# Sliding-window attention and a GELU layer on one core: seven products in place of eight in part of the first layer, and other places for the attention's visits

## Chip, core and metric

The kernel runs on one core of a Trainium2 chip. The metric is the device time of one execution in microseconds. The core's engines are TensorE (matrix products, "PE" in the profile, its weight loads "PEld"), VectorE ("DVE"), ScalarE ("ACT"), GpSimd ("POOL") and SyncE ("SP", which here only issues DMA transfers).

## What is computed

Windowed attention over 8 batches of 576 positions with 8 heads of 64, then two dense layers with a tanh GELU between them, over all 4608 positions:

```python
scores = scale * np.matmul(q, k.transpose(0, 1, 3, 2))
mask = np.abs(pos[:, None] - pos[None, :]) <= 32
scores = np.where(mask, scores, -1000000000.0)
attn = np.exp(scores - np.max(scores, axis=-1, keepdims=True))
attn = attn / (np.sum(attn, axis=-1, keepdims=True) + 1e-09)
x = np.matmul(attn, v)              # then reshaped to (4608, 512)
h = x @ w_in                        # (4608, 2048)
g = 0.5 * h * (1.0 + np.tanh(c * (h + 0.044715 * h * h * h)))
out = g @ w_out                     # (4608, 512)
```

## The kernel before

The positions go through the dense layers in nine tiles of 512. Each tile t has a first product (`ffn_in`, line 541: x by w_in, 16 columns of 128 features, four matmuls of 512 positions each) and a second product (by w_out). `gelu` (line 549) takes each of the 16 results out of PSUM on ScalarE. Tile 0 computes its second product directly (`ffn_out_0`). Tiles 1 to 8 compute it by Strassen-Winograd's seven products in place of eight (`ffn_out`, line 639; the table `WINO` gives the order: A11, S2, A12, S3, S1, A22, S4). The S factors are sums and differences of quarters of the GELU's result and are made by `sums` (line 584), four VectorE operations after every fourth column. The results are added up on VectorE in `ffn_out` and `ffn_last`, and stored from POOL's queue.

While tile t runs, the attention of batch t + 1 is computed between the matmuls of its second product. This order is written out by hand: `PLAN_0` (tile 0), `PLAN_1` (tile 1) and `PLAN` (tiles 2 to 6) map a step i of the second product (one matmul a step, 112 of them) to actions that are issued ahead of it:

- `s` scores of a pair of heads and their exponential (`score`, lines 436 and 448); `@0`, `@1` name the PSUM tile. `s-1` and group 4 are the tail, the last positions of a batch.
- `m` the mask (`mask`, line 454, VectorE).
- `v` the row sums and the product with V (`weigh`, lines 459 and 469), then on ScalarE the logarithm and the exponential that invert the sums (lines 494 and 495).
- `x` the normalizing product into xT on VectorE (`spread`, lines 504 and 510), which the first product of the next tile reads.
- in tile 0 also `d` (a second copy of a piece of V at shifted positions, lines 198 and 200), `e` (the cast of a piece of V on POOL), `n` and `p` (row sums and product with V of two pairs of heads), `w` and `u` (casts of w_out).

Three of 16 columns of the next tile's first product are begun at the end of a tile and finished at the start of the next. Each engine works strictly through its own instructions in the order in which they are written; between engines there are semaphores. ScalarE loads a table for the exponentials and another for the GELU. Tile 7 has only the tail of the last batch left (steps 5 and 31), tile 8 no attention at all.

q and k come in by SP's queue, v by POOL's (by SP's for the first three batches); q and k are cast on VectorE at the start of a tile and turned by transposing transfers on SP's queue (`cast_and_turn`, lines 364 and 386) into QT and KT, which `s0` needs.

[...]two of `psM` (`bank(0)`, `bank(1)`), two pairs of `psS` (tags S0 and S1, two banks each in one tile), and O and D of `psO`. In tiles 1 to 8 column n of the first product goes to bank 0, to the pair S0 (n = 1, 2) or, by n modulo 3, to D, bank 1 or bank 0.

Of the kernel before, what the change touches and what calls it, by code (L numbers as in the profile page):

```python
# [9 lines left out]
FP32 = mybir.dt.float32  # L10
FP16 = mybir.dt.float16
AF = mybir.ActivationFunctionType
ALU = mybir.AluOpType
# [23 lines left out]
def cut(b):  # L37
# [5 lines left out]

PLAN = {4: "s0@0 s1@1 v-1", 16: "m0 m1 x-1", 33: "s2@0 v0@1 v1", 36: "m2", 44: "x0", 50: "x1",
        62: "s3@0 s4@1 v2", 66: "m3", 80: "x2", 84: "m4", 91: "v3", 112: "x3"}


# [1 line left out]


PLAN_0 = {4: "s0@0", 9: "r1@1", 14: "s1@0", 15: "w1", 16: "m0", 19: "k2", 22: "r2@1", 23: "m1", 25: "s2@0", 27: "t-1@1",
          29: "w2", 31: "s-1@1", 33: "n0@0", 35: "e0", 36: "m2", 37: "k3", 38: "w5", 39: "m-1", 40: "r3@1", 43: "e1",
          45: "s3@0", 46: "v-1@1 d0", 47: "w3 e2", 48: "m3", 50: "d1", 51: "n2@0 x-1", 52: "e3 e4 d2", 54: "d3 p0@0",
          55: "u3 p2@1 x0 x1", 56: "x2 x3", 60: "c1"}
PLAN_1 = PLAN | {10: "s0@0", 12: "s1@1", 33: "s2@0", 40: "v0@1 v1", 50: "x0", 53: "x1", 57: "s-1@1", 62: "s3@0 v2",
                 63: "m-1", 66: "m3", 73: "v-1@1", 76: "x2", 80: "x-1", 86: "v3", 90: "s4@1", 98: "m4"}
PLAN_1[16] = "m0 m1"
for i in (4, 44, 84, 91):  # L60
    del PLAN_1[i]
PAIR_1 = {17: slice(0, 4), 40: slice(4, 8)}

ORDER_0 = [(t4, 4 * w + i) for w in range(3) for i in ((0, 2, 3, 1), (0, 2, 1, 3), range(4))[w] for t4 in (0, 1, 3, 2)] + \
# [8 lines left out]
def kernel(  # L73
# [264 lines left out]
    def bank(i):  # L338

        return psM.tile([128, 512], FP32, name="mm", tag=f"x{i}")  # L340
# [75 lines left out]

    def score(b, g, pair):
        m, prs, steps, slots, q0, n = work_of(b, g)
        ps = psS.tile([128, 2, 512], FP32, name="ps_s", tag=f"S{pair}")
        added = b == 0 and g < 4  # L420
        if added:
            for half in range(2):
                for h in range(2):
                    r0 = 64 * h
                    nc.tensor.matmul(ps[64 * half:64 * half + 64, h, :], idn[r0:r0 + 64, r0:r0 + 64],
                                     bias[half][r0:r0 + 64, :, :], start=True, stop=False,
                                     skip_group_check=True)
        for r, pr in enumerate(prs):
            for step in steps:
                for half, piece in enumerate(step):  # L430
                    if piece is None:
                        continue
                    k0, p0, p1 = piece
                    for h in range(2):
                        r0 = 64 * h
                        nc.tensor.matmul(  # L436
                            ps[64 * half:64 * half + 64, h, 4 * n * r:4 * n * r + 4 * n].rearrange(
                                "k (j p) -> k j p", j=4)[:, :, p0 - q0:p1 - q0],
                            KTs[b % 2][r0:r0 + 64, pr, k0:k0 + 64] if k0 < 512 else
                            KLs[b % 2][r0:r0 + 64, pr, :],  # L440
                            QTs[b][r0:r0 + 64, pr, :, p0:p1], start=not added, stop=True,
                            skip_group_check=added)
        w = 4 * n * len(prs)
        pe = yp.tile([128, 2, w], FP16, name="pe", tag="yo") if (b, g) == (1, 3) else \
            hp.tile([128, 2, w], FP16, name="pe", tag="qt16") if (b, g) == (0, 3) else \
            pep.tile([128, 2, w], FP16, name="pe", tag="pe") if g < 4 else \
            tailp.tile([128, 2, w], FP16, name="pet")
        nc.scalar.activation(pe, ps[:, :, 0:w], AF.Exp, scale=SCALE)  # L448
        groups[(b, g)] = pe

    def mask(b, g, hs=slice(0, 2)):
# [95 lines left out]
    def gelu(t, n):  # L547
        fc = column(t, n)
        nc.scalar.activation(gTs[t][:, fc, :], phs[fc], AF.Gelu_apprx_tanh)  # L549
        if t and n % 4 == 3:  # L550
            sums(t, n // 4)

    wino = {}

    def combine_w():
# [53 lines left out]
    def ffn_out_0(t4, fc):  # L609
        new = t4 not in pys  # L610
        if new:
            pys[t4] = bank(t4) if t4 < 2 else psO.tile([128, 512], FP32, name="py3", tag="OD"[t4 % 2])
        nc.tensor.matmul(pys[t4], gTs[0][:, fc, t4 * 128:t4 * 128 + 128], w_out16[:, fc, :],
                         start=new, stop=(fc == NF - 1))
        if fc == NF - 1:
            if "yo" not in pys:
                pys["yo"] = hp.tile([128, 2, 512], FP32, name="yo2", tag="qt16")
            yo = pys["yo"][:, t4, :] if t4 < 2 else yp.tile([128, 512], FP32, name="yo", tag="yo")
            (nc.scalar.copy if t4 > 1 else nc.vector.tensor_copy)(yo, pys[t4])
            later.append((t4, yo))  # L620

    def ffn_out(t, i):

        n, blk, f = i // 16, i // 8 % 2, i % 8
        a, w, new = WINO[n]
        end = t == NT - 1
        if i % 16 == 0 and new:
            pys[n % 2] = bank((1 + n) % 2)
            if end and n == 4:
                pys["apart"] = psO.tile([128, 512], FP32, name="py2", tag="O")  # L630
        py = pys[n % 2].rearrange("p (b c) -> p b c", b=2)
        apart = end and blk and n in (4, 6)
        if a[0] == "A":
            r0, c0 = 8 * (int(a[2]) - 1) + f, 256 * (int(a[1]) - 1) + 128 * blk
            lhsT = gTs[t][:, r0, c0:c0 + 128]
        else:
            lhsT = wino[a][:, f, 128 * blk:128 * blk + 128]
        one = end and n in (4, 6)
        nc.tensor.matmul(pys["apart"][:, 0:256] if apart else py[:, blk, :], lhsT,  # L639
                         wino[w][:, f, :], start=(new and i % (8 if one else 16) == 0),  # L640
                         stop=(i % (8 if one else 16) == (7 if one else 15)),
                         skip_group_check=True)
        if i % 16 < 15:
            return
        yo, left, right = wino["yo"], slice(0, 256), slice(256, 512)
        C11, C12, C21, C22 = (yo[:, r:r + 2, c] for r in (0, 2) for c in (left, right))

        M1, U2, U3 = C21, C12, C22
        if n == 0:
            nc.vector.tensor_copy(M1, py)  # L650
        elif n == 1:
            nc.vector.tensor_tensor(U2, py, M1, op=ALU.add)
        elif n == 2:
            (nc.vector.tensor_copy if t > 1 else nc.scalar.copy)(C11, py)
            if end:
                for x in range(2):
                    store(t, x, yo[:, x, :], left, nc.sync)
        elif n == 3:
            nc.vector.tensor_tensor(U3, py, M1, op=ALU.add)
        elif n == 4:  # L660
            if not end:
                nc.vector.tensor_tensor(C22, py, U3, op=ALU.add)
            else:
                for x, part in enumerate((py[:, 0, :], pys["apart"][:, 0:256])):
                    nc.vector.tensor_tensor(C22[:, x, :], part, U3[:, x, :], op=ALU.add)
                    store(t, 2 + x, yo[:, 2 + x, :], right, nc.sync, nc.scalar)
        elif n == 5:
            nc.vector.tensor_tensor(C21, py, M1, op=ALU.add)  # L668
            for x in range(2):
                store(t, 2 + x, yo[:, 2 + x, :], *((left, nc.sync, nc.scalar) if end else ()))  # L670
# [142 lines left out]
    for t in range(NT):  # L813
        b = t + 1
        att = b < B
        if t:
            for fc in range(begun):
                ffn_in(t, fc, 3, 4, then=False)
            for fc in range(begun):
                gelu(t, fc)  # L820
            if att and b > 1:
                parts = cast_and_turn(b)
            for fc in range(begun, NF):
                ffn_in(t, fc)
                if t == 1 and fc == 3:
                    parts[0]()
                    combine(4, nc.vector)
                if t == 1 and 6 <= fc < 10:
                    cast_v(2, fc - 6)
                if t == 1 and 9 <= fc < 14:  # L830
                    parts[1](fc - 9)
                if t == 1 and fc == 8:
                    trans_tails(1, psO.tile([128, 8, 128], FP16, name="pt", tag="O"))
                if t == 2 and fc in (8, 9):
                    store(0, *later[1 if fc == 8 else 3])
                if t > 1 and fc == 8 and att:
                    pair_v(b, nc.vector.tensor_copy)
        plan = PLAN_0 if not t else PLAN_1 if t == 1 else PLAN if att else {5: "v-1", 31: "x-1"} if t == B - 1 else {}

        def group(g):  # L840
            return (b, g) if g >= 0 else (b - 1, 4)
# [6 lines left out]
        for i in range(113 if t else 65):  # L848
# [3 lines left out]
            for act in plan.get(i, "").split():  # L852
# [56 lines left out]
                        load_table(gelu_set)  # L909
                else:  # L910
                    spread(*group(g), *ods[g])
            if t == 1 and i == 30:
                cast_vt(2)
                store(0, *later[0])
                store(0, *later[2])
# [42 lines left out]
```

## Time and profile before

| what | us |
|---|---|
| median of 11 runs | 302.69 |
| their range | 301.68 to 305.11 |
| the profiled execution | 308.77 |
| its span, first to last instruction | 307.1 |
| TensorE busy, matmuls | 291.1 |
| VectorE busy | 194.5 |
| ScalarE busy | 194.5 |
| POOL busy | 90.6 |
| tile 1 (from 57.86) | 32.95 |
| tile 2 (from 90.81) | 36.44 |
| tile 3 (from 127.25) | 31.28 |
| tiles 4, 5, 6 | 30.48, 30.42, 30.41 |
| tile 7 (from 249.84) | 26.81 |
| tile 8 (from 276.65) | 26.08 |

The span is that of one profiled execution; what lies around it is 1.67 us (308.77 - 307.1). The tiles' limits are the starts of the first product's begun columns. Busy time of TensorE counts pipelined matmuls; idle time of an engine costs something only where another one waits for it. In a row of the trace the number after the start is the duration, and square brackets give the idle time ahead of the first instruction of the row and what ended it.

### The profile page before, as it was taken

The page shows a single profiled execution, that of the slowest core. Times are in us where ns is not written, and L with a number is a line of the kernel's source. Part 1 is how long each engine was busy: PE and PEld are TensorE (multiplying, and loading weights), DVE is VectorE, ACT ScalarE, POOL GpSimd, SP SyncE. Part 2 cuts the span into 40 slices and gives each one's busy share as a digit, 9 for nine tenths or more (in the row PEclk, how much of TensorE's full clock was granted, in tenths as well). Part 3 has the DMA queues.
Part 4 walks back from the last instruction along what each step waited for, and adds up shares of the span by engine and source line. Part 5 has one row for each costly group of instructions (what it writes and reads, how often), then busy time and mean ns, then how long its engine had stood idle before and what let it go on. Part 6 is the DMA issues. An engine that isn't in the chain of part 4 may idle for free.

```text
span 307.1 us, 7125 instructions
## 1 busy us (share of the span) xinstructions
PE 291.1 (95%) x2893; PEld 180.7 (59%) x2893; DVE 194.5 (63%) x438; ACT 194.5 (63%) x307; POOL 90.6 (30%) x141
## 2 busy tenths in 40 slices
PE   7789999999899689998999999999999999999994
PEld 3434434446674368645864686468646864784583
DVE  4563576798776726885679577856786644632452
ACT  5965767679766637478647874787478747705600
POOL 3336316102754050510544414141530050006000
PEclk9999999999999959999999999999999999999998
DMA  7999998899799999298999896989597022004013
GB/s 223 262 284 383 341 278 239 224 195 188 204 201 195 211 254 166 80 104 125 243 182 178 206 190 128 153 208 181 100 166 95 2 51 89 2 0 138 2 34 103
DMA packets 116518, 50.73 MB, mean 165 GB/s; under 512 B 98007, under 2 KB 110039, under 8 KB 116486
## 3 DMA queue, kind: packets, MB, share of 16 engines
q1 hardware_dynamic: 87428, 37.88, 61.0%
q0 software_dynamic: 27936, 11.35, 25.4%
q10 hardware_dynamic: 1122, 1.06, 1.1%
q8 instruction: 22, 0.36, 0.6%
q14 instruction: 10, 0.08, 0.1%
HBM read 36.70 MB, written 9.44 MB: 150 GB/s over the span
## 4 chain that ended last, share of the span: by engine, by line
PE 64%; DMA 20%; SPq 6%; ACT 3%; DVE 3%; issue 1%; POOL 0%; DVEq 0%
PE mm L639 28%; PE mm L541 15%; PE ph L541 12%; DMA wst<-in_moe_w_out_dram 7%; DMA KT<-k 6%; DMA kr<-in_k_dram 5%; DMA wst<-in_moe_w_in_dram 3%; PE ps_s L436 3%; SPq L230 2%; PE ps_d L459 2%; SPq L176 2%; PE ps_o L469 2%; SPq L209 2%; ACT gT L549 1%; ACT pe L448 1%
## 5 line engine op out<-in xcount | busy, mean ns | idle before, releaser
L541 PEld LDWEIGHTS <-w_in 128*128 128x128 f16 x576 | 56.0, 98 | 66.3 <-DVE w_in L218 0.6
L541 PE MATMUL mm<-xT,w_in 128*128 128x512 f16 x304 | 74.7, 379 | 0.1
L549 ACT ACTIVATE gT<-mm 128x512 f16<-128x512 f32 x76 | 45.1, 597 | 40.0 <-PE mm L541 39.3
L541 PE MATMUL ph<-xT,w_in 128*128 128x512 f16 x272 | 68.2, 379 | 0.2 <-DVE w_in L218 0.2
L603 POOL DMA_DIRECT2D out_dram<-y x55 | 32.8, 605 | 94.0 <-DVE y L668 80.0
L639 PEld LDWEIGHTS <-s 128*128 128x128 f16 x512 | 49.8, 99 | 6.4
L584 DVE TENSOR_TENSOR s<-gT 128x512 f16<-128x512 f16 x64 | 26.8, 419 | 32.9 <-ACT gT L549 32.9
L549 ACT ACTIVATE gT<-ph 128x512 f16<-128x512 f32 x68 | 37.9, 599 | 12.8 <-PE ph L541 12.8
L639 PE MATMUL mm<-t,s 128*128 128x256 f16 x376 | 45.6, 275 | 0.0
L448 ACT ACTIVATE pe<-ps_s 128x960 f16<-128x960 f32 (+1 forms) x32 | 30.5, 976 | 19.6 <-PE ps_s L436 19.6
L639 PEld LDWEIGHTS <-gT 128*128 128x128 f16 x384 | 36.3, 99 | 7.3
L639 PE MATMUL mm<-w_out,gT 128*128 128x256 f16 x256 | 34.4, 280 | 0.0
L98 ACT ACT_TABLE_LOAD x18 | 23.1, 1283 | 2.2 <-issue 1.9
L494 ACT ACTIVATE lt<-ps_d 128x480 f32<-128x480 f32 (+2 forms) x28 | 15.5, 555 | 10.9 <-PE ps_d L459 7.0
L495 ACT ACTIVATE lt<-lt 128x480 f32<-128x480 f32 (+3 forms) x36 | 21.1, 585 | 1.1
L454 DVE TENSOR_TENSOR pe<-pe,band 128x960 f16<-128x960 f16 x28 | 18.5, 677 | 2.0 <-ACT pe L448 1.8
L469 PEld LDWEIGHTS <-V 128*64 128x64 f16 x520 | 14.4, 112 | 9.0 <-DVE V L194 2.2
L436 PE MATMUL ps_s<-QT,KT 64*64 64x128 f16 (+3 forms) x576 | 14.3, 221 | 4.9 <-DMA KT<-k 4.2
L184 POOL DMA_DIRECT2D V<-in_v_dram x20 | 17.9, 913 | 1.2 <-PE ps_o L469 0.4
L436 PEld LDWEIGHTS <-KT 64*64 64x64 f16 x576 | 10.4, 109 | 11.6 <-DMA KT<-k 5.0
L639 PE MATMUL mm<-t,gT 128*128 128x256 f16 x128 | 16.5, 273 | 0.0
L584 DVE TENSOR_TENSOR s<-s,gT 128x512 f16<-128x512 f16 x32 | 13.9, 434 | 1.1
(110 smaller groups left out, 324.0 us busy)
## 6 DMA issues: line engine op xcount, KB each, us to landing
kr<-in_k_dram SPq DMA_DIRECT2D x31, 256.0 KB, 11.1
qr<-in_q_dram SPq DMA_DIRECT2D x6, 1024.0 KB, 8.8
wst<-in_moe_w_in_dram SPq DMA_DIRECT2D x7, 512.0 KB, 8.2
V<-in_v_dram POOLq DMA_DIRECT2D x20, 128.0 KB, 8.5
wst<-in_moe_w_out_dram SPq DMA_DIRECT2D x2, 1024.0 KB, 10.9
wst<-in_moe_w_out_dram SPq DMA_DIRECT2D x4, 512.0 KB
qr<-in_q_dram SPq DMA_DIRECT2D x7, 256.0 KB, 7.1
out_dram<-y POOLq DMA_DIRECT2D x6, 192.0 KB, 5.9
```

Source lines behind the costliest of these rows:

```text
L98: nc.scalar.add_instruction(mybir.InstLoadActFuncSet(name=nc.get_next_instruction_name(), act_func_set_id=which, ins=[], outs=[]))
L184: nc.gpsimd.dma_start(V[:, c, :, :], v[b, :, 128 * c:128 * c + 128, :].rearrange("h p d -> p h d"))
L436: nc.tensor.matmul(ps[64 * half:64 * half + 64, h, 4 * n * r:4 * n * r + 4 * n].rearrange("k (j p) -> k j p", j=4)[:, :, p0 - q0:p1 - q0], ...
L448: nc.scalar.activation(pe, ps[:, :, 0:w], AF.Exp, scale=SCALE)
L454: nc.vector.tensor_tensor(pe, pe, m.rearrange("k (o j) p -> k o j p", o=1).broadcast_to(list(pe.shape)), op=ALU.mult)
L469: nc.tensor.matmul(o[64 * h:64 * h + 64, cols].rearrange("d (j p) -> d j p", j=4)[:, :, p0 - q0:p1 - q0], Vs[b % 2][:, slot, 2 * pr + h, : ...
L495: nc.scalar.activation(lt[:, 0:n], lt[:, 0:n], AF.Exp, scale=-1.0)
L541: nc.tensor.matmul(ph, w_in16[:, dc, fc * 128:fc * 128 + 128], xT[:, dc, t * 512 % RING:t * 512 % RING + 512], start=(dc == 0), stop=(dc = ...
L549: nc.scalar.activation(gTs[t][:, fc, :], phs[fc], AF.Gelu_apprx_tanh)
L584: nc.vector.tensor_tensor(dst, x, y, op=op)
L603: eng.dma_start(out_v[b, j, q0 + p:q0 + p + e, cols], yo[m:m + e, cols])
L639: nc.tensor.matmul(pys["apart"][:, 0:256] if apart else py[:, blk, :], lhsT, wino[w][:, f, :], start=(new and i % (8 if one else 16) == 0) ...
```

## The change

Three things are changed.

1. **Plans.** In tile 1 the nine steps at which TensorE leaves the second product for attention (10, 12, 33, 40, 57, 62, 73, 86, 90) become four (12, 45, 69, 91). `s2` is scored into the banks O and D, in two exponentials. In tiles 2 to 6 the first visit moves from step 4 to step 7. In tile 0 `d1` stands ahead of the mask `m3`, `x-1` behind `d3`, `p0` and `p2` come in one visit, the cast of V's tail (`e4`) comes after `u3`.
2. **Copies.** The result copies of tile 0's blocks 0 and 1, 2 and 3 are divided otherwise between ScalarE (now 0 and 3) and VectorE; tile 1's copy of C11 goes to VectorE.
3. **First product of tiles 7 and 8.** Eight of the 16 columns (two units A and B of four columns each) are computed by the same seven products, each of four matmuls of 256 positions (`in_step`). Their w_in combinations are made once on POOL (`in_w`), those of x on VectorE (`in_x`). `MIX` is the order: numbers are ordinary columns, `A0` is product 0 of unit A. Products 0, 1, 3, 5 of a unit add up in one bank: after 0 the bank is copied by VectorE, after 1 and 3 by ScalarE, after 5 the GELU reads it. Product 2 is added to the copy of 0, and 4 and 6 add up in a third bank and are added to the copies of 3 and 1. A2 and B0 share the pair S1, A4 and B4 the pair S0.

```diff
-PLAN = {4: "s0@0 s1@1 v-1", 16: "m0 m1 x-1", 33: "s2@0 v0@1 v1", 36: "m2", 44: "x0", 50: "x1",
+PLAN = {7: "s0@0 s1@1 v-1", 16: "m0 m1 x-1", 33: "s2@0 v0@1 v1", 36: "m2", 44: "x0", 50: "x1",
...
-          29: "w2", 31: "s-1@1", 33: "n0@0", 35: "e0", 36: "m2", 37: "k3", 38: "w5", 39: "m-1", 40: "r3@1", 43: "e1",
-          45: "s3@0", 46: "v-1@1 d0", 47: "w3 e2", 48: "m3", 50: "d1", 51: "n2@0 x-1", 52: "e3 e4 d2", 54: "d3 p0@0",
-          55: "u3 p2@1 x0 x1", 56: "x2 x3", 60: "c1"}
-PLAN_1 = PLAN | {10: "s0@0", 12: "s1@1", 33: "s2@0", 40: "v0@1 v1", 50: "x0", 53: "x1", 57: "s-1@1", 62: "s3@0 v2",
-                 63: "m-1", 66: "m3", 73: "v-1@1", 76: "x2", 80: "x-1", 86: "v3", 90: "s4@1", 98: "m4"}
+          29: "w2", 33: "s-1@1 n0@0", 35: "e0", 36: "m2", 37: "k3", 38: "w5", 39: "m-1", 40: "r3@1", 43: "e1",
+          46: "s3@0 v-1@1 d0", 47: "w3 e2", 48: "d1 m3", 51: "n2@0", 52: "e3 d2 d3 x-1",
+          55: "u3 p0@0 p2@1 x0 x1", 56: "e4 x2 x3", 60: "c1"}
+MIX = "3 A0 A2 B0 B2 A1 A4 B1 B4 12 A3 B3 13 A5 B5 A6 B6 14 15".split()
+UNITS = {"A": 1, "B": 2}
+PLAN_1 = {12: "s0@0 s1@1 s2", 16: "m0 m1", 36: "m2", 45: "v0@1 v1 s-1@0", 52: "x0", 55: "x1", 62: "m-1",
+          69: "s3@0 v2 v-1@1", 73: "m3", 81: "x2", 85: "x-1", 91: "v3 s4@1", 112: "x3 m4"}
...
+    def in_w(unit, *which):
...
+        for x in which:
+            dst, a, b, op = ((S1, A21, A22, ALU.add), (S2, S1, A11, ALU.subtract),
+                             (S3, A11, A21, ALU.subtract), (S4, A12, S2, ALU.subtract))[x - 1]
+            nc.gpsimd.tensor_tensor(dst, a, b, op=op)
+    def in_x(t):
...
+        for dst, a, b in ((T1, B12, B11), (T2, B22, T1), (T3, B22, B12), (T4, B21, T2)):
+            nc.vector.tensor_tensor(dst, a, b, op=ALU.subtract)
+    def in_step(t, unit, n):
...
+        if n in (0, 2, 4):
+            if (unit, n) == ("A", 0):
+                bank_of = psO.tile([128, 512], FP32, name="pu", tag="O")
+            elif (unit, n) == ("B", 2):
+                bank_of = bank(0)
+            else:
+                if unit == "A":
+                    mixed["ps"] = psS.tile([128, 2, 512], FP32, name="pu2", tag="S1" if n == 2 else "S0")
+                bank_of = mixed["ps"][:, 0 if unit == "A" else 1, :]
...
+        for h in range(2):
+            for d in range(2):
+                nc.tensor.matmul(ps[:, h, :], lhs[:, d, 128 * h:128 * h + 128], rhs[:, d, :],
...
+        def total(x, r, c):
+            nc.vector.tensor_tensor(x, ps, x, op=ALU.add)
+            out_of(x, r, c)
+        if n == 0:
+            nc.vector.tensor_copy(s1, ps)
+        elif n == 2:
+            total(s1, 0, 0)
+        elif n == 1:
+            nc.scalar.copy(s2, ps)
+        elif n == 3:
+            nc.scalar.copy(s3, ps)
+            if unit == "B":
+                for u in "AB":
+                    x = mixed[u][:, 2]
+                    nc.vector.tensor_tensor(x, phs[u, "c"], x, op=ALU.add)
...
+        elif n == 5:
+            out_of(ps, 1, 0)
+        elif n == 6:
+            total(s2, 0, 1)
+            sums(t, i)
...
-            (nc.scalar.copy if t4 > 1 else nc.vector.tensor_copy)(yo, pys[t4])
+            (nc.scalar.copy if t4 in (0, 3) else nc.vector.tensor_copy)(yo, pys[t4])
...
-            (nc.vector.tensor_copy if t > 1 else nc.scalar.copy)(C11, py)
+            nc.vector.tensor_copy(C11, py)
...
+            if t > 6:
+                if t == 7:
+                    in_x(7)
+                    in_w("A", 3)
+                    in_w("B", 3)
+                    in_w("A", 4)
+                    in_w("B", 4)
+                for step in MIX:
+                    if step[0] in UNITS:
+                        in_step(t, step[0], int(step[1]))
+                    else:
+                        ffn_in(t, int(step))
...
+            if t == 7 and i == 60:
+                in_x(8)
+            if t == 6 and i == 92:
+                in_w("A", 1, 2)
+                in_w("B", 1, 2)
```

Here `out_of` is the GELU (128 by 512, ScalarE) that writes a quarter of a unit's result, and `sums` the four VectorE combinations of the kernel before, which now follow A6, B6 and the columns 3 and 15.

## The prediction

> **What bounds the kernel now.** I read the page first (busy shares, then the chain that ended last), then the busy time by stage, then TensorE's waits one by one, and last the rows of VectorE and ScalarE inside tile 7, where the largest part of the change sits.
>
> ```profile
> PE 291.1 (95%) x2893; PEld 180.7 (59%) x2893; DVE 194.5 (63%) x438; ACT 194.5 (63%) x307; POOL 90.6 (30%) x141
> ...
> PE 64%; DMA 20%; SPq 6%; ACT 3%; DVE 3%; issue 1%; POOL 0%; DVEq 0%
> ```
>
> TensorE is the bound from tile 1 on; the DMA share of the chain lies in tile 0 (weights) and at one place in tile 2. By stage, one row for each of tiles 1 to 4, 7 and 8 (length, busy time of TensorE's matmuls, its weight loads, VectorE, ScalarE and POOL; then TensorE's granted clock, the DMA share and GB/s):
>
> ```profile
> 57.86:90.81 32.95, 32.11 (x351) 20.28 (x351) 26.18 (x55) 26.73 (x42) 9.90 (x15) 1.00 1.06 194
> 90.81:127.25 36.44, 33.03 (x332) 21.50 (x330) 22.21 (x50) 21.55 (x33) 10.71 (x17) 0.91 1.26 180
> 127.25:158.53 31.28, 30.48 (x331) 20.01 (x330) 22.17 (x49) 21.55 (x33) 9.60 (x15) 1.00 1.18 163
> 158.53:189.01 30.48, 30.48 (x332) 20.05 (x330) 22.54 (x53) 21.55 (x33) 11.16 (x17) 1.00 1.10 176
> 249.84:276.65 26.81, 26.67 (x188) 17.61 (x186) 11.45 (x25) 12.81 (x20) 4.27 (x8) 1.00 0.14 40
> 276.65:302.73 26.08, 26.04 (x177) 17.04 (x174) 11.48 (x26) 9.23 (x16) 4.93 (x9) 1.00 0.22 63
> ```
>
> Tile 4 is gapless at 30.48 us; tile 1 has 2.5 us above it. Tiles 7 and 8 have no slack in them: what another engine delays there, the end of the kernel is delayed by. Tile 2 is 6 us longer than tile 4 because of one wait and what it does to the clock. The wait, and then four stretches of one length (TensorE's busy time, its granted clock):
>
> ```profile
> 108.48 1.02 PE L436 MATMUL ps_s<-QT,KT 64*64 64x96 f16 x32 [3.41 <-DMA KT<-k]
> ```
> ```profile
> 103.69:107.10 3.41, 1.38 (x9) 1.00 1.36 183
> 107.10:110.51 3.41, 2.03 (x44) 0.50 1.00 216
> 110.51:113.93 3.42, 3.42 (x18) 0.50 1.21 299
> 14.95:18.36 3.41, 2.21 (x24) 1.00 1.00 237
> ```
>
> The clock fell to half at 107.1, after a stretch of 3.41 us in which TensorE was busy for 1.38, and came back at 113.9. A stretch with 2.21 busy did not bring it down. The profiled execution took 308.77 us against a median of 302.69. Its 6.1 us too many are about this wait (3.41) and the half clock behind it (first visit of tile 2 to its second 6.88 us, in tile 3 4.34: 2.5). So I take it that the median runs have little of either, and set the sum on the profiled time less 6.1.
>
> Last, the start of tile 7's first product, in order of time on ScalarE and VectorE:
>
> ```profile
> 252.04 0.60 ACT L549 ACTIVATE gT<-mm 128x512 f16<-128x512 f32 x1 [2.29 <-PE mm L541]
> 252.53 1.57 ACT L549 ACTIVATE gT<-ph 128x512 f16<-128x512 f32 x3
> ```
> ```profile
> 254.14 0.42 DVE L584 TENSOR_TENSOR s<-gT 128x512 f16<-128x512 f16 x1 [3.50 <-ACT gT L549]
> ...
> 255.28 0.42 DVE L584 TENSOR_TENSOR s<-gT,s 128x512 f16<-128x512 f16 x1
> ```
>
> The first four gelus end at 254.10; the first of the combinations (four per `sums`) runs 254.14 to 255.70, though TensorE finished that fourth product at 253.29. Today nothing waits for it.
>
> [...]
>
> **Tiles 7 and 8, the new product.** Removed: 8 of 16 columns, 32 matmuls of 512 columns at 0.216 us (8 take 1.73 in the chain), 6.91 us. Added: 14 steps of four 256-column matmuls at 0.109 (72 take 7.86), 6.11 us. Without a stall TensorE gains 0.8 us per tile. Added on VectorE per tile: two copies out of PSUM and six totals at 0.69 us (the L654 and L659 rows of tile 7), and four differences of x at 0.42 (the L584 row); on ScalarE four copies at 0.57 to 0.59. VectorE had 5.3 us of work in 13.8, so capacity is there. The order is what counts. I walk through it from the tile's start (249.84 = 0), taking each duration from the rows above, 0.05 us from one engine's end to the next one's start, and a spacing of 0.5 for back-to-back ScalarE and 0.6 for back-to-back VectorE work on PSUM, as the trace has them.
> - TensorE: three begun columns and column 3 to 3.46, A0 to 3.89, A2 to 4.33. B0 is written into the two-bank tile whose other half A2 filled, and in the built program its first matmul waits until VectorE has read A2.
> - VectorE: the combinations of columns 0 to 3 stand ahead of the copy of A0 and so run first, 4.30 to 5.86. Copy of A0 to 6.5; total of A2, which needs that copy, to 7.23. B0 starts at 7.28: a gap of 2.95 us.
> - B0, B2, A1, A4, B1, B4, 12, A3, B3, 13, A5, B5, A6 then follow to 13.8 without a gap that matters. B6 waits for A6's total (13.82 to 14.51): a gap of 0.8. Then 14 and 15 to 16.7.
> - The gelu of 14 stands on ScalarE behind that of B6's total; this total stands on VectorE behind A's four combinations, which wait for the gelu of A6's total (to 15.86; behind 13's and A5's and B5's). Combinations to 17.4, total to 18.1, gelu to 18.7, gelu of 14 to 19.2, of 15 to 19.7.
> - The second product starts at 16.7. In tile 7 `v-1` at step 5 needs the bank that 15's gelu frees: a gap of 2.5 (before: 0.25). In tile 8 step 7 needs 14's gelu, a gap of 1.8; then 0.3 for the last combinations and 0.2 for the first copy out, which comes late behind them.
>
> Sum: tile 7 2.95 + 0.8 + 2.25 - 0.8 = +5.2; tile 8 2.95 + 0.8 + 1.8 + 0.5 - 0.8 = +5.2. Together +10.4, nothing after it in either tile that could take it back.
>
> The clock comes on top. A gap of 2.95 leaves at most 1.9 us of work in one of the two windows it touches, mostly less: within 1.38 in about two thirds of the positions, and between that and 2.21 in the rest, where the trace decides nothing. I take one half-clock window for each tile, 1.7 us of work lost, +3.4; bounds 0 and 6.8 (two windows each, as in tile 2).
>
> GpSimd's eight combinations of w_in have no row. [...] The first four are issued in tile 6, where POOL is idle from 225 to 249; the other four come behind tile 6's stores (249.1 to 253.6)[...]. They hide, but lie beside the first combinations on VectorE: 0 to 1.5 us more in tile 7; I take 0.5.
>
> **Tile 0.** The second copies of V (d1, d2) no longer stand behind the last mask and the tail's product. TensorE's gaps ahead of the last visit are 0.37, 0.23 and 0.37, the chain there is VectorE's. The last cast of V ends at 52.9, d3's two copies take 0.7, so `p0` could start at 53.65 in place of 54.33: -0.7, and up to -0.3 more from ScalarE taking the first copy out, for which the next tile waited (57.60 to 57.86). The cast of V's tail goes behind another cast on POOL; it is used in tile 1 only.
>
> **Tile 1.** Of the 2.5 us above tile 4, 0.66 is a wait for V's copies at `v0` (78.12 to 78.77), 0.2 a wait for the bank of `s-1`, 0.2 the transposes of the tail; 1.4 is left for five visits more. The two matmuls between the first two visits take 0.32 us in place of 0.22, so a visit costs between 0.1 and 0.28; I take 0.2. The wait for V stays and holds both kernels at 78.75, where the new one is five matmuls further (0.55); of tile 0's gain nothing gets past it. From there it has three visits less (0.6) and no bank wait (0.2): -1.3 at the end of tile 1, bounds -0.5 and -2.3 (V earlier as well). Hidden: C11's copy goes from ScalarE to VectorE (0.69, which is free for 6.8 us of tile 1), `s2`'s exponential in two halves is 0.2 longer on ScalarE, and the last mask moves behind `x3`, used 4 us later.
>
> **Tiles 2 to 6, first visit at step 7.** Where K's transposes are late, three matmuls (0.33 us) come ahead of the wait: 0.3 to 0.7 in a run like the profiled one. Elsewhere nothing: the exponentials wait for the table load (to 174.29 in tile 4), 1 us after the scores; V's loads stay at step 4, and no transfer changes its place on SP's queue. But the earlier end of tile 1 meets the same wait. The transposes of Q and K are issued behind casts that run at the start of tile 2 and so move with it, the loads of K (landed at 95.28) don't. Between none and all of the 1.3 passes; I take 1.0 with 0.3 from the step: -1.3 in all for tiles 0 to 6.
>
> **Sum.** 308.77 - 6.1 + 10.4 + 3.4 + 0.5 - 1.3 = 315.7 us. A profile taken with tile 2's wait in it would be some 6 longer.
>
> **Rivals.**
> - The queue walk holds, the clock does not fall: 312.3, with the tail of the gains 311. For it: the gap is shorter than tile 2's 3.41. Against: 1.38 us of work did not save the clock there. 0.28.
> - It falls for two windows a tile, or a second time at the gap before the second product (2.5 in a window): 319. 0.14.
> - The faster side: VectorE gets the copy of A0 out in time. This decides at 4.33 in the walk: if its queue has A2 read by then, no gap arises, both tiles gain 0.8, and it is 302.7 - 1.6 - 1.3 = 299.8. Against: four gelus in series end at 4.26 in the trace, and the copy stands behind what they feed. 0.05.
> - The gaps are a third of what I walk through and the clock stays: about 303, no change. 0.03.
>
> The forecast has 0.50. Range: the low end is the walk without clock, less a tenth, with the larger gains of tiles 0 and 1 (309.5), the high end two windows in each tile (320). Less than 0.5% either way (1.5 us) can't be told from no change: faster 0.05, same 0.03, slower 0.92.
>
> **What would show it.** In tile 7 and 8: a gap on TensorE of about 3 us ahead of B0, released by VectorE's total; a second of some 2 us at step 5 (tile 7) and 7 (tile 8), released by a gelu; half the clock after the first; 31 to 34 us for tile 7 in place of 26.81. In tile 1: 31.3 to 31.8 in place of 32.95, the wait for V still there. I am wrong if B0 follows A2 at once, or if tiles 7 and 8 are shorter than 27.

## The result, and the profile after

The changed kernel takes 320.73 us (median of 12 runs, 318.50 to 329.56) against 302.79 us for the kernel before on the same chip (47 runs): a ratio of 1.058, 95% interval 1.056 to 1.061. It is slower by 18 us. Ratios and their intervals leave out runs more than 1.5% above the fastest of their kernel, here three of the 12; medians are of all runs. The direction was predicted, the size was not: 315.7 was forecast, with a range up to 320.0.

The profiled execution of the changed kernel took 318.5 us (span 316.8). Its page, busy time first, then the chain that ended last by engine:

```profile
PE 290.9 (92%) x2941; PEld 186.2 (59%) x2941; DVE 215.6 (68%) x463; ACT 196.6 (62%) x315; POOL 98.7 (31%) x149
...
PE 63%; DMA 15%; DVE 9%; SPq 6%; ACT 5%; issue 1%; POOL 1%; DVEq 0%
```

TensorE is busy for as long as before (291.1), in a span that is 9.7 us longer. VectorE has 21.1 us more work for 25 instructions more, which is 0.84 us each, though none of the new ones takes over 0.69 us undisturbed. And VectorE's share of the chain has gone from 3% to 9%. Busy time by stage, with the same columns as before, for tiles 1, 2, 3, 7 and 8:

```profile
57.01:89.25 32.24, 31.33 (x352) 20.62 (x350) 25.91 (x56) 25.16 (x41) 10.09 (x17) 1.00 1.07 195
89.25:119.66 30.41, 30.41 (x332) 20.05 (x330) 22.04 (x50) 21.77 (x34) 10.77 (x16) 1.00 1.26 212
119.66:150.08 30.42, 30.42 (x333) 20.04 (x331) 22.05 (x49) 21.55 (x34) 9.38 (x15) 1.00 1.24 180
241.39:279.18 37.79, 28.04 (x212) 20.79 (x210) 23.08 (x41) 14.40 (x25) 8.91 (x13) 0.91 0.10 29
279.18:312.48 33.30, 27.94 (x202) 20.13 (x199) 16.65 (x34) 10.76 (x20) 4.91 (x9) 0.95 0.18 50
```

Cut at the same instructions (from tile 2 on 0.16 us ahead of the limits in the table of before), the profile of before has 57.86 us ahead of tile 1 (now 57.01), 32.79 for tile 1, 36.44 for tile 2, 31.28 for tile 3, 26.81 for tile 7 and 26.21 for tile 8. So tile 7 costs 10.98 us and tile 8 7.09. Tiles 0 and 1 gain 0.85 and 0.55. Tiles 2 and 3 are 6.03 and 0.86 shorter, but for another reason: this execution met no listed wait for the transfer of K, where before waited 3.41 and 0.80. All of it together is +9.7, which is the difference of the two profiled executions.

TensorE's waits (what it waited for: us in total, times, longest), and then the places in tiles 7 and 8 in order of time:

```profile
PE pu L609 <- DVE sa L618: 11.3, 4, 6.8
PE ps_d L469 <- ACT gT L559: 2.2, 1, 2.2
PE mm L728 <- ACT gT L559: 1.5, 1, 1.5
```
```profile
252.63 1.01 PE L609 MATMUL pu<-xT,w_in 128*128 128x256 f16 x4 [6.75 <-DVE sa L618]
...
261.95 0.60 PE L609 MATMUL pu<-xT,wc 128*128 128x256 f16 x4 [0.78 <-DVE sa L618]
...
267.03 0.35 PE L469 MATMUL ps_d<-pet,ones 128*64 128x384 f16 x2 [2.22 <-ACT gT L559]
...
286.64 0.61 PE L609 MATMUL pu<-xT,w_in 128*128 128x256 f16 x4 [2.97 <-DVE sa L618]
...
295.81 0.60 PE L609 MATMUL pu<-xT,wc 128*128 128x256 f16 x4 [0.78 <-DVE sa L618]
...
300.42 1.16 PE L728 MATMUL mm<-w_out,gT 128*128 128x256 f16 x9 [1.51 <-ACT gT L559]
```

All predicted places are there: ahead of B0, ahead of B6, and at the second product. In tile 8 the gap ahead of B0 is 2.97 us where the walk through the queues gave 2.95. In tile 7 the same gap is 6.75. What stands behind it is one VectorE instruction and four of GpSimd (POOL):

```profile
245.85 4.21 DVE L673 TENSOR_TENSOR s<-gT 128x512 f16<-128x512 f16 x1 [2.04 <-ACT gT L559]
250.09 0.43 DVE L673 TENSOR_TENSOR s<-s,gT 128x512 f16<-128x512 f16 x1
```
```profile
245.29 2.27 POOL L578 TENSOR_TENSOR wc<-w_in 128x512 f16<-128x512 f16 x2
247.52 2.25 POOL L578 TENSOR_TENSOR wc<-w_in,wc 128x512 f16<-128x512 f16 x2
```

The first of the combinations for the second product takes 4.21 us; the next one, of the same shape, takes 0.43. The long one ends 0.3 us after the last of GpSimd's four. The copy of A0 and the total of A2 stand behind the four combinations in VectorE's order and ran at 251.10 and 251.89, though the matmuls of both had ended at 245.88; B0 waits for that total.

The clock, in stretches of one length through tile 7 and then tile 8:

```profile
245.78:249.19 3.41, 0.10 (x1) 0.00 (x0) 3.34 (x1) 0.03 (x1) 3.41 (x4) 1.00 0.44 141
249.19:252.61 3.42, 0.00 (x0) 0.00 (x0) 3.25 (x6) 0.00 (x0) 0.57 (x1) 0.55 0.00 0
252.61:256.02 3.41, 3.39 (x17) 2.33 (x17) 1.38 (x2) 1.39 (x3) 0.00 (x0) 0.50 0.00 0
...
283.32:286.74 3.42, 0.45 (x5) 0.26 (x3) 2.81 (x6) 0.40 (x2) 0.77 (x2) 1.00 0.67 199
286.74:290.15 3.41, 3.41 (x19) 2.50 (x18) 1.38 (x2) 1.62 (x3) 0.00 (x0) 0.55 0.02 5
```

The clock fell some 0.35 us behind the limits chosen here, which is why the mixed stretches show 0.55. Tile 7 has it at half for two such lengths (6.83 us), but in the first of them TensorE has only the last 0.33 us of work and loses next to nothing. So each tile loses about one stretch's worth of work, as predicted.

### The profile page after: what moved, and what is told of

Read it like the earlier page. It is cut to its first block, busy times and chain, and to the rows that moved or that the text cites. A ratio compares the mean times of both kernels' runs of the same rounds, so it can differ in the third digit from the quotient of the medians.

```text
span 316.8 us, 7268 instructions
## 1 busy us (share of the span) xinstructions
PE 290.9 (92%) x2941; PEld 186.2 (59%) x2941; DVE 215.6 (68%) x463; ACT 196.6 (62%) x315; POOL 98.7 (31%) x149
## 4 chain that ended last, share of the span: by engine, by line
PE 63%; DMA 15%; DVE 9%; SPq 6%; ACT 5%; issue 1%; POOL 1%; DVEq 0%
PE mm L728 28%; PE mm L551 13%; PE ph L551 11%; DVE s L673 5%; DMA tr<-in_q_dram 3%; DMA qr<-in_q_dram 3%; DMA wst<-in_moe_w_in_dram 3%; DMA wst<-in_moe_w_out_dram 3%; PE ps_s L442 3%; PE pu L609 2%; ACT gT L559 2%; SPq L234 2%; PE ps_d L469 2%; DMA qr<-in_v_dram 2%; PE ps_o L479 2%; SPq L213 1%
## 5 line engine op out<-in xcount | busy, mean ns | idle before, releaser
L551 PEld LDWEIGHTS <-w_in 128*128 128x128 f16 x512 | 49.8, 98 | 57.6 <-DVE w_in L222 0.6
L551 PE MATMUL ph<-xT,w_in 128*128 128x512 f16 x256 | 64.1, 379 | 0.5 <-POOL w_in L844 0.4
L551 PE MATMUL mm<-xT,w_in 128*128 128x512 f16 x256 | 63.7, 379 | 0.0
L559 ACT ACTIVATE gT<-mm 128x512 f16<-128x512 f32 x64 | 37.9, 596 | 36.2 <-PE mm L551 35.7
L673 DVE TENSOR_TENSOR s<-gT 128x512 f16<-128x512 f16 x64 | 32.5, 507 | 19.6 <-ACT gT L559 15.6
L559 ACT ACTIVATE gT<-ph 128x512 f16<-128x512 f32 x64 | 35.5, 599 | 12.5 <-PE ph L551 12.5
L728 PE MATMUL mm<-w_out,gT 128*128 128x256 f16 x256 | 33.0, 273 | 1.5 <-ACT gT L559 1.5
L505 ACT ACTIVATE lt<-lt 128x480 f32<-128x480 f32 (+3 forms) x36 | 21.1, 586 | 1.1
L673 DVE TENSOR_TENSOR s<-s,gT 128x512 f16<-128x512 f16 x32 | 15.2, 475 | 1.1
L728 PE MATMUL mm<-w_out,s 128*128 128x256 f16 x120 | 14.4, 273 | 0.0
L673 DVE TENSOR_TENSOR s<-gT,s 128x512 f16<-128x512 f16 x32 | 14.3, 448 | 0.0
```

The lines of the kernel that those rows point to most:

```text
L505: nc.scalar.activation(lt[:, 0:n], lt[:, 0:n], AF.Exp, scale=-1.0)
L551: nc.tensor.matmul(ph, w_in16[:, dc, fc * 128:fc * 128 + 128], xT[:, dc, t * 512 % RING:t * 512 % RING + 512], start=(dc == 0), stop=(dc = ...
L673: nc.vector.tensor_tensor(dst, x, y, op=op)
```

## The experiments

The theory after this: the queue walk and the clock are as predicted, and what is missing in the sum is GpSimd's work on w_in, which holds VectorE up. The rivals: the long gap belongs to the queues and GpSimd only happens to run then; or the changed plans of tiles 0 to 6 cost something in place of gaining. Length of tiles 2, 6, 7 and 8 in the profile of each kernel, in us, for all that follows:

| kernel | tile 2 | tile 6 | tile 7 | tile 8 |
|---|---|---|---|---|
| before | 36.44 | 30.42 | 26.81 | 26.21 |
| after | 30.41 | 30.42 | 37.79 | 33.30 |
| 1, plans alone | 33.23 | 30.46 | 26.81 | 26.20 |
| 2, GpSimd early | 37.90 | 33.29 | 32.20 | 33.30 |
| 3, front reordered | 34.14 | 33.29 | 31.30 | 29.06 |
| 4, front and end | 30.42 | 33.28 | 27.53 | 27.69 |
| 5, w_in on VectorE | 31.99 | 30.41 | 33.87 | 33.29 |
| 6, reordered, VectorE | 34.96 | 30.50 | 27.52 | 27.67 |
| 7, sums split | 35.68 | 30.50 | 27.51 | 27.68 |
| 8, before, late scores | 30.51 | 30.41 | 26.81 | 26.21 |
| 9, plans, late scores | 34.75 | 30.42 | 26.81 | 26.20 |

**1. The plans alone.** The new first product is left out, and tiles 7 and 8 compute it as before:

```diff
-            if t > 6:
+            if t > 8:
...
-            for fc in range(begun, NF if t < 7 else 0):
+            for fc in range(begun, NF):
...
-            if t == 7 and i == 60:
-                in_x(8)
-            if t == 6 and i == 92:
-                in_w("A", 1, 2)
-                in_w("B", 1, 2)
```

> Left out: the new first product of tiles 7 and 8; the plans and copies of tiles 0 to 6 as changed. My theory: they save 1.3 us, 301.5 (300.5 to 302.5), tile 1 at about 32.4, tiles 7 and 8 at 26.8 and 26.1 as before, and the new product costs the whole of the rest, some 19 us. Rival one: what tiles 0 and 1 save is swallowed by the waits for V and K, 302.8 and no difference from before. Rival two: the plans themselves cost several us and the product less than its two tiles show, 304 or more.

Measured: 301.84 us (14 runs, 298.85 to 307.77) beside 301.83 for before; ratio 0.996, 0.992 to 0.999. The plans cost nothing that shows, so the 18 us are all in the new first product. Whether they gain is less clear: the ratio says a little, but the medians are equal, and the means of all runs are 302.51 and 302.26. Its profile has a wait at tile 2 that the profile of after doesn't have, so part of the gain can have come back as this wait:

```profile
PE ps_s L442 <- DMA KT<-k: 2.7, 1, 2.7
```

**2. GpSimd's eight combinations together, in tile 6.** The four that ran at tile 7's start are issued with the other four at step 92 of tile 6:

```diff
-                    in_w("A", 3)
-                    in_w("B", 3)
-                    in_w("A", 4)
-                    in_w("B", 4)
...
-                in_w("A", 1, 2)
-                in_w("B", 1, 2)
+                in_w("A", 1, 2, 3, 4)
+                in_w("B", 1, 2, 3, 4)
```

> The changed kernel, with all eight combinations of w_in on GpSimd in tile 6, step 92, none at the start of tile 7. Theory of contention (VectorE's first combination took 4.21 us in place of 0.42 because GpSimd was reading SBUF with four combinations from 245.29 to 249.77): the first combination of tile 7 is back at 0.42, TensorE's gap ahead of B0 in tile 7 falls from 6.75 to 3.0 as in tile 8, one half-clock window in place of two; 3.8 to 5.5 us faster than the changed kernel, 315 to 317. Rival (the order of the queues alone makes the gap, and the long combination is its wait): the gap stays near 6.7 and the time at 320.7.

Measured: 322.78 us (4 runs), ratio 1.067, 1.060 to 1.073: no gain at all. Tile 7 did become 5.6 us shorter, and its gap ahead of B0 fell to 2.97. But tile 6 is 2.9 us longer. GpSimd has no wait ahead of these eight, so they don't run at step 92, they run from 5.9 us into tile 6, behind the stores (224.33 to 234.56), beside VectorE's combinations of that tile. VectorE, GpSimd, and then TensorE there:

```profile
224.08 1.70 DVE L673 TENSOR_TENSOR s<-s,gT 128x512 f16<-128x512 f16 x1
225.71 1.37 DVE L673 TENSOR_TENSOR s<-gT 128x512 f16<-128x512 f16 x1
227.00 1.37 DVE L673 TENSOR_TENSOR s<-gT,s 128x512 f16<-128x512 f16 x1
```
```profile
225.57 1.23 POOL L578 TENSOR_TENSOR wc<-wc,w_in 128x512 f16<-128x512 f16 x1
226.76 1.33 POOL L578 TENSOR_TENSOR wc<-w_in 128x512 f16<-128x512 f16 x1
```
```profile
236.53 0.39 PE L728 MATMUL mm<-t,s 128*128 128x256 f16 x2 [0.85 <-DVE s L673]
238.00 1.26 PE L728 MATMUL mm<-t,s 128*128 128x256 f16 x10 [1.07 <-DVE s L673]
```

Here the two engines' instructions start in turn. VectorE's seven combinations in this stretch took 1.26 to 1.70 us each in place of 0.42, GpSimd's eight 1.16 to 1.33. The interference was moved to another tile, not taken away. In the changed kernel, too, GpSimd's first four run early in tile 6 (216.90 to 221.96), and VectorE's combinations took 1.37 to 1.70 us there, but TensorE loses nothing by it (tile 6 is 30.42 us long):

```profile
216.65 1.70 DVE L673 TENSOR_TENSOR s<-s,gT 128x512 f16<-128x512 f16 x1
218.28 1.37 DVE L673 TENSOR_TENSOR s<-gT 128x512 f16<-128x512 f16 x1
```
```profile
216.90 1.17 POOL L578 TENSOR_TENSOR wc<-w_in 128x512 f16<-128x512 f16 x1
```

The rest of the missing gain is, in this profile, a wait of 5.0 us for K at tile 2, the same transfer as in the first experiment, with 6.83 us at half clock from inside it on.

**3. Matmuls ahead of the reads, at the front.** On top of the second experiment: B0's matmuls are issued ahead of the total of A2 that they stood behind (`A2-` is a step's matmuls, `A2+` its reads), and the combinations of columns 0 to 3 (`q0`) come after the first reads. Only the order is shown; the lines that carry it out are left out:

```diff
-MIX = "3 A0 A2 B0 B2 A1 A4 B1 B4 12 A3 B3 13 A5 B5 A6 B6 14 15".split()
+MIX = "3 A0 A2- B0- A2+ B0+ B2 q0 A1 A4 B1 B4 12 A3 B3 13 A5 B5 A6 q1 B6 q2 14 15 q3".split()
```

> As the one with early GpSimd work, and in both tiles the four combinations of columns 0 to 3 stand on VectorE behind the copies and totals of A0, A2, B0 and B2, and B0's matmuls are issued ahead of the read of A2. Theory of the queue: no gap ahead of B0, so 3.0 us less in each tile, and no half clock after it (1.7 each): 6 to 9.5 us less than with early GpSimd work alone, 306 to 310; the gap ahead of B6 and that at the second product stay. Rival (B0's wait is for PSUM or for the weights' combinations): the gap of 3 us stays.

Measured: 313.06 us (4 runs), ratio 1.028, 1.020 to 1.036. The gap ahead of B0 is gone from both tiles, and tile 8 is 4.2 us shorter (2.97 of gap and the half clock behind it). That is the queue walk's first gap, confirmed by taking it away. Tile 7 is only 0.9 us shorter, since the clock now fell there behind the 2.21 us gap at the second product, which it had not done in the second experiment. Some 3.8 us of the difference between the two profiles are tile 2's, by a shorter wait for K, and have nothing to do with the edit.

**4. The end as well.** A6 and B6 are treated in the same way, and B6's total stands ahead of A's combinations (`q1`):

```diff
-... A5 B5 A6 q1 B6 q2 14 15 q3".split()
+... A5 B5 A6- B6- A6+ B6+ q1 q2 14 15 q3".split()
```

> As the one before, and A6 and B6 are both issued ahead of their totals, B6's total ahead of A's combinations. Theory of the queue: the gap of 0.8 us ahead of B6 goes, the gelus of 14 and 15 come some 1.5 us earlier, so the gaps of 2.2 us (tile 7) and 1.5 us (tile 8) at the second product fall below 1; 3 to 4 us less than the kernel with the front mended alone, 303 to 306. Rival (ScalarE's own load makes those gaps): less than 1 us gained.

Measured: 307.18 us (4 runs), ratio 1.021, 1.014 to 1.028; tiles 7 and 8 are down to 27.53 and 27.69. The gap ahead of B6 is gone, the one at tile 7's second product is 0.83 in place of 2.21, and tile 8 has 1.03 for a combination, one product later, in place of 1.51; the clock doesn't fall (1.00 granted in both tiles). What is left above before in this profile is 2.9 us in tile 6, where GpSimd's eight still stand beside VectorE, and 0.7 and 1.5 in tiles 7 and 8.

**5. The same work on VectorE.** One word of the changed kernel differs:

```diff
-            nc.gpsimd.tensor_tensor(dst, a, b, op=op)
+            nc.vector.tensor_tensor(dst, a, b, op=op)
```

> The kernel after with one word changed: the eight combinations of w_in are made by VectorE in place of GpSimd, at the same places of the program (S1 and S2 at step 92 of tile 6, S3 and S4 behind tile 7's sums of x). Theory (GpSimd's four combinations in a row held VectorE's first combination in tile 7 for 4.21 us and brought a second half-clock window, 3.8 + 1.7 us above the 0.42 us of an undisturbed one): tile 7's wait of TensorE before its fourth group falls from 6.75 to about 3 us, tile 7 is some 5.5 us shorter, and the time about 315 us, 5.5 under the changed kernel's 320.7, ratio to before about 1.04. Four more VectorE instructions of 0.42 us stand in tile 7 ahead of the first read; they lie beside TensorE's seven first groups. Rival (the long wait in tile 7 is a queue behind something else, a copy or a gelu, and GpSimd only happens to run then): the wait stays above 6 us and the time within 1 us of 320.7.

Measured: 314.93 us (4 runs; before 302.14 beside it), ratio 1.046, 1.038 to 1.053. The first combination of tile 7 takes 0.42 us, and the gap ahead of B0 is the one of tile 8:

```profile
245.88 0.42 DVE L673 TENSOR_TENSOR s<-gT 128x512 f16<-128x512 f16 x1 [0.48 <-ACT gT L559]
```
```profile
248.88 0.73 PE L609 MATMUL pu<-xT,w_in 128*128 128x256 f16 x4 [2.97 <-DVE sa L618]
```

The rival is out: with four instructions more in VectorE's own queue the queues alone make 2.97, and GpSimd made the other 3.78. Tile 7 is 3.92 us shorter, of which 3.78 is the gap; I had expected 5.5, with a second stretch at half clock. As the stretches above show, that stretch held hardly any work. The two ratios differ by 0.013, which is 3.9 us as well, give or take 2.3 by their intervals. This is the price of the interference in the changed kernel, in one place.

**6. The reordered kernel with w_in on VectorE.** The fourth kernel with the combinations on VectorE (the word of the fifth experiment), in the gaps of its row in tile 6:

```diff
-            if t == 6 and i == 92:
-                in_w("A", 1, 2, 3, 4)
-                in_w("B", 1, 2, 3, 4)
+            if t == 6 and i in (68, 82, 96, 106):
+                for unit in "AB":
+                    in_w(unit, (68, 82, 96, 106).index(i) + 1)
```

> The kernel of the fourth experiment (matmuls of A2, B0, A6 and B6 issued ahead of the reads they were queued behind, the combinations of the second product set apart from them) with the eight combinations of w_in on VectorE, two at each of steps 68, 82, 96 and 106 of tile 6, where VectorE's row shows gaps of 0.5 to 1.7 us. Theory (GpSimd's eight slow VectorE's combinations in tile 6 from 0.42 to 1.26-1.71 us, and TensorE's two waits of 0.85 and 1.07 us in tile 6's second product come from it): those two waits are gone, tile 6 is about as long as tile 5 but for at most 0.5 us, and the profile is about 300 us, 2 to 3 us under the fourth experiment's 302.8; ratio to before 0.99 to 1.00. Rival (VectorE has no room in tile 6, so the combinations come back as waits of TensorE on VectorE at its end or at tile 7's start): a wait of 1 to 3 us appears there, and the ratio is 1.00 to 1.01.

Measured: 303.48 us (22 runs), ratio 1.005, 1.002 to 1.007. Tile 6 is back at 30.50, as the theory has it, with eight instructions more on VectorE. The ratio lies where the rival put it, but no wait of the rival's kind is there. What remains fits the tiles: 7 and 8 are still 0.7 and 1.5 us longer than before, and less the 1.4 of the plans that is 0.8 us, where the interval is 0.6 to 2.2. Tile 2, which this experiment doesn't touch, took 34.96 us in its profile, with a wait for K. Tiles 6, 7 and 8:

```profile
214.71:245.21 30.50, 30.50 (x332) 20.02 (x330) 23.62 (x55) 21.62 (x34) 6.42 (x11) 1.00 0.48 76
245.21:272.73 27.52, 26.59 (x213) 19.86 (x211) 19.97 (x44) 14.03 (x24) 4.47 (x9) 1.00 0.14 39
272.73:300.40 27.67, 26.41 (x202) 19.24 (x199) 16.45 (x34) 10.45 (x20) 4.89 (x9) 1.00 0.21 60
```

TensorE's busy time in tiles 7 and 8 is 26.59 and 26.41 us; before it was 26.67 and 26.20. So no saving shows in the busy time. The starts of the matmuls tell more: from the first of tile 7's first product to the first of its second it is 13.62 us here (245.21 to 258.83), and 13.81 before. The 256-column matmuls follow one another at 0.109 us, as predicted, but B1, A3, B3 and A6 begin 0.23, 0.20, 0.06 and 0.13 us late. That is 0.61 us of the 0.8, in pieces too short for the lists of waits.

**7. The sums split.** S1 and S2 of the last three groups ahead of all S3 and S4, and tile 7's last visit later:

```diff
-... A6- B6- A6+ B6+ q1 q2 14 15 q3".split()
+... A6- B6- A6+ B6+ q1 q2 14 15 q3 r1 r2 r3".split()
...
-{5: "v-1", 31: "x-1"}
+{14: "v-1", 31: "x-1"}
```

> The sixth experiment's kernel, and the last two waits of tiles 7 and 8 taken on: the second product's S1 and S2 of the last three groups are all made ahead of S3 and S4, which are read later, and tile 7's last visit is moved from step 5 to step 14 of the second product. Theory (the 1.03 us wait in tile 8 is for S2 of the last group, which stands behind six S3 and S4 it doesn't need; the 0.83 us in tile 7 is for the bank of the last gelu): both waits go, 1.5 to 2 us under the sixth experiment, profile about 298 us, ratio 0.985 to 0.99. Rival (S2 of the last group waits for its own gelu): the wait in tile 8 stays above 0.7 us, and the time within 1 us of the sixth experiment.

Measured: 306.38 us (6 runs), ratio 1.011, 1.005 to 1.017. Tiles 7 and 8 are as long as in the sixth experiment, so they don't explain a median 2.9 us higher; this profile has a wait of 3.8 us for K at tile 2. Both waits went, and others came in their place, 0.64 us in tile 7 and 1.21 in tile 8:

```profile
PE mm L729 <- DVE y L740: 1.9, 2, 1.2
```

The copy of the second product's first result (line 740) now stands behind the combinations that were put off, and the third product needs its bank. Neither of the two theories had this: in tile 8 VectorE's row is all but unbroken from 287.19 to 292.27, and in this experiment another order only made another reader late.

**8. The kernel before, with tile 2's score visits late.** Its first visit stands at step 28 of tile 2:

```diff
+PLAN_2 = {7: "v-1", 16: "x-1", 28: "s0@0 s1@1", 37: "m0 m1", 50: "s2@0 v0@1 v1", 54: "m2", 60: "x0", 66: "x1",
+          72: "s3@0 s4@1 v2", 76: "m3", 88: "x2", 92: "m4", 96: "v3", 112: "x3"}
...
-PLAN_1 if t == 1 else PLAN if att
+PLAN_1 if t == 1 else PLAN_2 if t == 2 else PLAN if att
```

> The kernel before with tile 2 alone changed: its first two score visits stand at step 28 of the second product in place of step 4, and the visits behind them are spread over what is left, so that the transposes that write K of batch 2 have some 2.6 us more to land. Theory (TensorE's wait for that transfer at tile 2 is up to 5 us long and differs from run to run; it makes the spread of the runs, and brings half-clock windows): the wait falls by what is given, 2.6 us, tile 2 is 31 to 34 us long in place of 33 to 37, and the time falls by 1.5 to 3 us, ratio 0.990 to 0.995. Rival (the visits pushed together at tile 2's end, or the transfer landing later still, give it back): ratio 0.998 to 1.003.

Measured: 302.28 us (22 runs, 301.12 to 303.29) beside 302.33 (39 runs, 301.35 to 308.79); ratio 0.998, 0.996 to 1.000. The median doesn't move, so the rival's number is right, but not its mechanism: nothing is given back in tile 2, which took 30.51 us:

```profile
89.99:120.50 30.51, 30.51 (x332) 20.04 (x330) 22.34 (x51) 21.03 (x33) 10.85 (x17) 1.00 1.33 207
```

What goes is the upper end of the runs, 5.5 us of it. So, by the spread of the runs, the wait for K is an event of some executions, and most runs of the kernel before have little of it.

**9. The plans alone, with the same late visits.** The first kernel with the `PLAN_2` of the eighth.

> The first experiment's kernel (the changed kernel with its new first product left out, so the plans of tiles 0 and 1 and step 7 alone) with the same late visits in tile 2. Theory (tiles 0 and 1 end 1.3 us earlier, but the transfer of K of batch 2 doesn't land earlier for it, so in most runs the gain comes back as wait at tile 2): with the wait covered, the gain shows, and this is 1 to 1.5 us under the eighth experiment, ratio to before 0.985 to 0.990. Rival (the plans gain nothing by themselves beyond what the first experiment's 0.9958 shows against before): this and the eighth experiment are within 0.5 us of each other.

Measured: 301.19 us (18 runs, 299.95 to 306.32), ratio 0.995, 0.993 to 0.997. That is 1.1 us under the eighth experiment by the medians, about the size that tiles 0 and 1 show in the profile (1.4), though the two intervals still overlap by a little, and the 0.985 to 0.990 against before were not reached, since the late visits themselves gain next to nothing. In its profiled execution, the longest of its runs, tile 2 took 34.75 us and tile 3 32.47, with a wait of 2.0 us for K in each: 2.6 us more time doesn't always cover the wait. This is the fastest version by its ratio, half a per cent under the kernel before.

## Why the prediction was wrong

By its own steps:

- **The queue walk (5.2 us a tile): right, by errors that cancel.** Predicted gaps 2.95 and 0.8, measured 2.97 and 0.78 in tile 8. At the second product 2.5 was predicted for tile 7 and 2.22 measured, 1.8 and 0.5 for tile 8 and 1.51 measured. Of the term "without a stall TensorE gains 0.8 us per tile" 0.2 was left in the sixth experiment; the rest went in late starts of B1, A3, B3 and A6, 0.06 to 0.23 us each, which the walk took for "without a gap that matters". In tile 8 the smaller last gap and the missing gain cancel, and the tile is 7.09 longer, where 5.2 and 1.7 make 6.9.
- **The clock (1.7 us a tile): right, in tile 7 with luck.** That the stretches have fixed limits was taken, not shown, ahead of the result; the last section has what the profiles show of it. One stretch of 3.41 us at half clock was full of work in each of tiles 7 and 8. Tile 7 had two, but the first was all but empty. There the clock fell behind a gap of 6.75 us; behind one of 2.97, as walked through, it fell in the fifth experiment and not in the second.
- **GpSimd beside the first combinations ("I take 0.5", 0 to 1.5): the step that failed.** It measured 3.9 us. The bound was the author's estimate: no row of before has a GpSimd combination, alone or beside VectorE. The second four took 4.5 us (245.29 to 249.77), 1.1 each, in the place predicted; the first four ran not between 225 and 249 but at 216.9 to 222.0, which cost TensorE nothing. A bound of 1.5 leaves room for little more than one of them, but VectorE's instruction was held for all four, 4.21 us. The walk had what was needed to see the overlap: it put the four behind the stores (from 3.8 us into the tile; they ran from 3.9 to 8.4) and the first combination at 4.30 (it started at 4.46). For their length the profile of before had GpSimd's casts of w_in, also 128x512, at 0.87 us each (line 218): four of those from 3.8 on end at 7.3, by estimate an overlap of 3.0 us, where 3.9 were measured. And it had the copy of A0 and the total of A2, for which B0 waits, behind that one instruction. The bound should have been what was left of GpSimd's four, not the length of one.
- **Tiles 0 to 6 (−1.3): right in the profile (−1.4), not seen whole in the median.** Tile 0 gained 0.85 (0.7 predicted), tile 1 0.55. The way there was not the predicted one: the wait for V in tile 1, which was to hold both kernels at 78.75, was there (0.84 us) but ended at 78.20, so part of tile 0's gain did get past it. Over all profiles shown here tile 2 starts at 87.7 to 89.3 us in the nine with the new plans, and at 90.0 and 90.7 in the two with the old. In the first experiment the interval of the ratio holds this gain (0.1 to 0.8%), the median shows none; the ninth has 1.1 us of it.
- **The sum.** 3.4 of the 5.0 us missing are the GpSimd term. With its parts as measured, 302.79 + 10.98 + 7.09 − 1.40 is 319.5. The remaining 1.3 us is not settled. The runs show tile 2's wait for K in some executions and not in others; an earlier end of tile 1 meets it sooner, and part of the plans' gain can go there (not shown). The interval of the ratio alone is 1.8 us wide.
- **The base.** The profiled execution of before was set down by 6.1 us for tile 2. The eighth experiment, with that wait covered, ran at 302.28, the base was 302.67.

The high end of the range, 320.0, was put on the clock alone, two windows in each tile. The unknown cost that was really open, an operation with no row beside a queue with no slack, had been bounded by the length of one instruction.

## What to carry to other kernels

Instructions put on a second engine because that engine was idle had a price on its neighbour here, 3.78 us of TensorE's wait in tile 7: bound such a price by the length of the whole run of such instructions, not by one, and ask what stands behind the neighbour's instruction at that moment. Work issued late in the program of an engine with nothing to wait for ran early, at 5.9 us into tile 6 though it was issued at step 92: look where it lands. And a product with fewer multiplications has to earn its extra copies and totals where they share the queue that the next matmul waits for; here the best order found still was 0.7 to 1.5 us a tile behind the plain product.

## What the runs showed of the hardware that was not expected

- The VectorE combination (128x512, f16) that started at 245.85 in tile 7, 0.56 us into GpSimd's run of four, took 4.21 us in place of 0.42 and ended at 250.06, behind the last of the four; in tile 6, both in the changed kernel and in the second experiment, the two engines' instructions started in turn, with 1.26 to 1.70 us for each of VectorE's. What decides between the two was not tried.
- A copy within SBUF was longer too: the copy of V (64 x 2048, f16) took 1.55 us in the second experiment beside the last of GpSimd's eight, and 0.69 in the profile of after, when its four were over.
- The clock fell on a grid in these profiles: in that of after at 249.55 and 287.09, 11 times 3.413 us apart, in that of before at 107.12 and 305.09, 58 times. With the two profiles cut on their grids, the clock fell after the full-clock windows with 1.36 and 1.02 us of TensorE's busy time in before and 0.00 and 0.45 in after, and after none of the others, which held 2.21 or more in before and 1.49 or more in after. Between 1.36 and 1.49 these two decide nothing. What counts inside a window was not tried.
- So it mattered where a gap lay against the grid. In the second experiment the gap of 2.97 us ahead of B0 in tile 7 was divided between two windows with 2.03 and 1.82 us of work, and the clock stayed (tile 7 is 5.4 us longer than before, the walk without the clock). In tile 8 the same gap lay in one window with 0.44, and it fell. The gap of 2.2 us at tile 7's second product left 1.62 us in its window in the changed kernel, and the clock stayed; in the third experiment it left 1.20, and it fell.
